# Two attention and gated-MLP layers on one core: score blocks tied to slots, products in column parts, weights transposed by their loads, and more units for VectorE

## The chip, the cores and the metric

The kernel runs on one core of a Trainium2 chip. A core has a matrix engine (TensorE, "PE" in the profile; its weight loads are shown as "PEld"), ScalarE ("ACT"), VectorE ("DVE"), GpSimd ("POOL") and a queue engine (SyncE, "SP") that issues the DMA transfers. The metric is the device time of one execution in microseconds (us). The kernel before took 1782.1, 1781.82 and 1775.51 us in three runs, a median of 1781.82 us.

## The reference, cut to what matters

There are 2048 tokens of width 512. Two layers follow each other with the same weights. Each layer is an attention part with 32 query heads of 16 elements that share one key and one value head, and then a gated MLP whose gate mixes the tokens with a 2048 x 2048 matrix `w_sp`.

```
scores = jnp.einsum('bhqd,bkd->bhqk', q, k) * Dh ** (-0.5)
p = _softmax(scores, axis=-1)
o = jnp.einsum('bhqk,bkd->bhqd', p, v)
...
z = _gelu(jnp.einsum('bsd,df->bsf', x, w_in))
z1 = z[..., :Fh].copy()
z2 = _layernorm(z[..., Fh:], axis=-1)
g = jnp.einsum('ts,bsf->btf', w_sp, z2) + b_sp[None, :, None]
return jnp.einsum('bsf,fd->bsd', z1 * g, w_out)
...
x = x + _A_ref(_layernorm(x, axis=-1), A_wq, A_wk, A_wv, A_wo)
x = x + _B_ref(_layernorm(x, axis=-1), B_w_in, B_w_sp, B_b_sp, B_w_out)
```

The softmax needs an exponential for each of 32 x 2048 x 2048 scores in each layer. In the kernel this is the largest piece of element work.

## The kernel before, in words

**Units, blocks and slots.** The scores of a layer are cut into 32 *groups* (2048 query rows each, counted over heads and tokens), and a group into 16 *units*, one for each tile of 128 keys. A unit is four *blocks* of 128 keys x 512 queries; block j lies in row part j of the array, because the contraction is only 32 rows deep (16 elements, and 16 that are zero). `scores` issues the matmul of one block with `tile_position=(32 * j, 0)`. Matmuls in different row parts run beside each other.

**Who makes the exponentials.** Most units go to ScalarE: `push_unit` queues their blocks, and `push_slot` puts them, three and two in turn, into two PSUM *slots* (banks 0 to 2 and 3 to 4); one `activation` call (line 805) turns a whole slot into probabilities in `P_ring`. `push_pv` then multiplies the unit's four blocks with the values (line 822), in four column parts of the array, into bank 6. Some units go to VectorE instead (`push_unit_dve`): each of the four blocks gets a bank of its own from the two *side banks* 5 and 7, line 853 turns the scores into 16-bit integers, four integer additions (line 862) make four shifted copies, and read as bf16 numbers the five copies, weighted by `PH_W`, sum to the exponential. Their product with the values (line 868) takes five sets of four matmuls where a ScalarE unit takes one. `ON_DVE` and `UNITS` say which units of a group go to VectorE: none in the first four groups (apart from `FIRST_DVE`), three of 16 in the next 20, two in the next four, one in the last four. That makes 152 of the 1024 units of both layers.

**The order of the work.** The program is first written as a graph of operations with priorities and estimated durations (`_Graph.op`), and `schedule` plays it through before anything is emitted, with the constants at the head of the file. Each engine then executes its own list strictly in that order, with semaphores between the engines (`emit`). On PE a set of up to four small matmuls, or one full 128 x 128 matmul, is charged 0.217 us for 512 columns. Each operation has a `mode`: 1 for row parts (scores), 2 for column parts (values), 0 for the full array, and a change of mode is charged 0.105 us. Where PE would be idle for long, `filler` puts in matmuls with ones or zeros (lines 613, 618 and 621) that change no result. The matmuls of a product are added in pieces by `products`; their banks are the side banks.

**Around the attention.** While the attention runs, the rest of the layer runs at lower priority: `q_slot` (queries, line 751), `wo_tiles` (output projection, line 950), `b_front` (the MLP's input products, lines 1020 and 1039), and `mix_stage` (the mixing of the tokens in three stages of four token tiles, line 1146, with sums parked in device memory, `gp_d`). After the last group of a layer, `mix_late` does the last stage (line 1185), the gating (line 1194) and the output product (line 1198). In the first layer this is interleaved with the first keys and scores of the second layer, and in the second layer it is the end of the kernel.

**The mixing matrix.** The product needs `w_sp` with its two dimensions swapped. In the first layer `turn_wsp` loads 16 row tiles of 512 KB, transposes them on PE (256 matmuls with the identity, line 1245), copies them out of PSUM on VectorE (32 copies, line 1248) and stores them to `wspt_scratch` in device memory. `mix_stage` (line 1127) and `mix_late` (line 1162) load from there, with 40 loads in both layers together. The weights `wo`, `w_in` and `w_out` are loaded between the row tiles (`load_weights`).

Of the kernel before, what the change touches and what calls it, by code (L numbers as in the profile page):

```python
# [17 lines left out]
KD = 4  # L18
# [86 lines left out]
class _Graph:  # L105
# [66 lines left out]
    def schedule(self):  # L172
# [81 lines left out]
        def pick(e):  # L254
# [7 lines left out]
            for ent in ready[e]:  # L262
# [3 lines left out]
                p = ent[0] - (0.95 if e == "pe" and o.mode == last_mode else 0.0)  # L266
                if beside(o):
                    p -= 2.0
# [191 lines left out]
def bass_interleave_layers__grouped_kv_mqa__mixer_gmlp__prompt_kernel(  # L460
# [98 lines left out]
    z1flat = z1c[:].rearrange("p f s -> p (f s)")  # L559
    wsp_stage = z1flat[:, 0:2 * S].rearrange("p (b s) -> p b s", b=2)  # L560
    wsp_tile = z1flat[:, 2 * S:4 * S].rearrange("p (b t q) -> p b t q", b=2, q=P)
    Z1ALL = [("z1", f, t) for f in range(NF1) for t in range(NT)]

    wspT_d = nc.dram_tensor("wspt_scratch", [NT, P, S], BF16)
    wspT_dv = wspT_d.ap().rearrange("st p t -> p st t")
# [22 lines left out]
    def dve(fn, us, r, w, prio=5):  # L588
        return op("dve", fn, us, r=r, w=w, prio=prio)

# [56 lines left out]
    def load_weights(i):  # L647

        rd = [("wd", 2 * i + 1)]
        if i == 0:  # L650
            dma(lambda e: e.dma_start(wo_r[:], A_wo.rearrange("(c p) n -> p c n", p=P)), rd, ["wo"], "wo", 6.0)
        elif i == 1:
            dma(lambda e: e.dma_start(w_in_r[:], B_w_in.rearrange("(kd p) f -> p kd f", p=P)), rd, ["w_in"], "win", 10.0)
        elif i == 2:
            dma(lambda e: e.dma_start(w_out_r[:], B_w_out.rearrange("(c p) n -> p c n", p=P)), rd, ["w_out"], "wout",
                10.0)
# [85 lines left out]
    def q_slot(si, pr=3):  # L742
# [5 lines left out]
        def mk(e, k):  # L748
            u, kd = k // KD, k % KD
            c = g // 2 * m + u  # L750
            return e.matmul(bank32(tk.bank)[:, u * w:(u + 1) * w], wq_r[:, kd, c * P:(c + 1) * P],  # L751
                            xnTA[:, kd, t0 * P:t0 * P + w], start=(kd == 0), stop=(kd == KD - 1))
        products(tk, m * KD, mk, lambda k: [("xa", k % KD, t) for t in range(t0, t0 + n)] + ["wq"], pr,
                 us=w * MM + 0.01)
# [7 lines left out]
    main = {"blocks": [], "i": 0, "s": 0, "pv": [], "last": None}  # L762
    SLOTS = ((0, 3), (3, 2))

    def push_unit(u):

        main["pv"].append([u, 4])
        for j in range(4):
            main["blocks"].append((u, j))
# [14 lines left out]
    def push_slot(n):  # L784
# [3 lines left out]
        main["i"] += 1  # L788
        b0 = SLOTS[i][0]
# [12 lines left out]
        o.rows = frozenset(j for _, j in blocks)  # L802

# [12 lines left out]
    def push_pv(u, places):  # L816
        hg, kt, first, last, done = u

# [6 lines left out]
        pv_op(pe_pv, [("P", s) for s, _ in places] + [("V", kt)], first, last, TILED)  # L825
        if last:
            done()
# [12 lines left out]
    def push_unit_dve(u):  # L840

        hg, kt, first, last = u[:4]
        assert not first and not last
        tiles = [phr["base"] + (phr["n"] + a) % NRING for a in range(NPH)]
        phr["n"] += NPH
        first_op = None
        for j in range(4):
            tk = _Task()
            o = op("pe", lambda e, j=j, tk=tk: scores(e, bank32(tk.bank), u, j), TILED, r=[("K", hg[1], kt), ("q", hg[0])],
                   w=[tk], prio=P_S, lat=PE_LAT, mode=1)  # L850
            o.work = TILED / 4
            o.rows = frozenset((j,))
            o = dve(lambda e, j=j, tk=tk: e.tensor_scalar(  # L853
                ph16[:, tiles[0], j * QC:(j + 1) * QC], bank32(tk.bank), PH_BIAS, 0.0, op0=ALU.add, op1=ALU.max),
                0.66, [tk], BIG(tiles[0]) if j == 0 else [("phj", tiles[0], j)], P_R)
            if j == 0:
                first_op = o
            else:
# [417 lines left out]
    for layer in range(2):  # L1276
        now["layer"] = layer
        phr["base"] = 8 - NRING
        for t0, n in KEYS:
# [12 lines left out]
            if not layer and t0 == 0:  # L1292
                for tt in range(NT):
                    turn_wsp(tt)
                    if tt % 2:
                        load_weights(tt // 2)
# [40 lines left out]
```

## Time and profile before

| what | value |
|---|---|
| runs | 1782.1, 1781.82 and 1775.51 us (median 1781.82) |
| span of the profiled execution | 1773.4 us; the page gives no other time for this execution |
| PE busy | 1689.0 us (95%), 15326 matmuls |
| ScalarE busy | 1663.7 us (94%), 1586.3 us of it the exponentials of line 805 |
| VectorE busy | 1355.8 us (76%) |
| GpSimd busy | 92.1 us (5%) |
| DMA | 133.00 MB, mean 75 GB/s |

The span runs from the first to the last instruction, so it lies a little below the times of the runs. A busy PE is not PE at its peak: matmuls are pipelined, and each record includes the time that it takes to pass through the array, so the time from one start to the next says more than a duration. The same holds for the exponentials, whose records overlap: 698 calls of 1528 ns and 696 calls of 1108 ns would be more than the 1586.3 us in which the engine was busy with them. "Idle before" is the time an engine stood still ahead of a group of instructions, with what ended it.

### The profile page before, as it was taken

The page shows a single profiled execution, that of the slowest core. Times are in us where ns is not written, and L with a number is a line of the kernel's source. Part 1 is how long each engine was busy: PE and PEld are TensorE (multiplying, and loading weights), DVE is VectorE, ACT ScalarE, POOL GpSimd, SP SyncE. Part 2 cuts the span into 40 slices and gives each one's busy share as a digit, 9 for nine tenths or more (in the row PEclk, how much of TensorE's full clock was granted, in tenths as well). Part 3 has the DMA queues.
Part 4 walks back from the last instruction along what each step waited for, and adds up shares of the span by engine and source line. Part 5 has one row for each costly group of instructions (what it writes and reads, how often), then busy time and mean ns, then how long its engine had stood idle before and what let it go on. Part 6 is the DMA issues. An engine that isn't in the chain of part 4 may idle for free.

```text
span 1773.4 us, 35455 instructions
## 1 busy us (share of the span) xinstructions
PE 1689.0 (95%) x15326; PEld 556.9 (31%) x15326; DVE 1355.8 (76%) x2450; ACT 1663.7 (94%) x1448; POOL 92.1 (5%) x145
## 2 busy tenths in 40 slices
PE   8899999999999999999999999999999999999999
PEld 4332322232333232233433222322232332322333
DVE  8679787888888877544677886888888887765647
ACT  7999999999999999999588999999999999999980
POOL 2000000000000000000322000000000000000012
PEclk9999999999999999999999999999999999999999
DMA  5840100011000223555420000001200003244474
GB/s 159 228 109 1 49 1 1 25 64 34 7 13 7 88 92 114 179 178 175 138 75 25 1 2 1 2 1 37 78 25 1 13 14 104 80 164 156 144 251 164
DMA packets 112044, 133.00 MB, mean 75 GB/s; under 512 B 41104, under 2 KB 68112, under 8 KB 111888
## 3 DMA queue, kind: packets, MB, share of 16 engines
q1 hardware_dynamic: 111888, 130.74, 22.8%
q8 instruction: 120, 1.97, 0.4%
q14 instruction: 36, 0.29, 0.0%
HBM read 76.19 MB, written 54.53 MB: 74 GB/s over the span
## 4 chain that ended last, share of the span: by engine, by line
ACT 77%; PE 20%; DVE 2%; DMA 1%; issue 1%; POOL 0%; SPq 0%; DVEq 0%
ACT P_ring L805 73%; PE ps_all L781 5%; PE ps_all L822 2%; PE ps_all L1146 2%; PE ps_all L1198 2%; PE ps_all L868 2%; PE ps_all L1185 1%; PE ps_all L1020 1%; ACT z2n L1063 1%; ACT z1c L1088 1%; PE ps_all L621 1%; ACT L805 1%; ACT L1063 1%; DMA z1c<-in_B_w_sp_dram 0%; PE ps_all L751 0%
## 5 line engine op out<-in xcount | busy, mean ns | idle before, releaser
L805 ACT ACTIVATE P_ring<-ps_all 128x1536 bf16<-128x1536 f32 (+1 forms) x1396 | 1586.3, 1317 | 58.2 <-PE ps_all L781 56.4
L781 PE MATMUL ps_all<-qT,kT_rep 32*128 32x512 bf16 x4096 | 640.4, 385 | 67.8 <-ACT P_ring L805 51.4
L853 DVE TENSOR_SCALAR big<-ps_all 128x512 int16<-128x512 f32 x608 | 400.0, 685 | 45.5 <-PE ps_all L781 40.0
L862 DVE TENSOR_SCALAR big<-big 128x2048 int16<-128x2048 int16 x608 | 396.9, 682 | 24.9 <-PE ps_all L868 23.6
L781 PEld LDWEIGHTS ps_all<-qT,kT_rep 32*128 32x128 bf16 x4096 | 159.1, 91 | 587.4 <-ACT P_ring L805 449.1
L822 PE MATMUL ps_all<-P_ring,V_aug 128*32 128x512 bf16 x3488 | 340.5, 390 | 2.1 <-DVE oT L916 1.1
L868 PE MATMUL ps_all<-big,V_ph 128*32 128x512 bf16 x3040 | 251.2, 388 | 0.6 <-DVE big L853 0.4
L1149 DVE TENSOR_TENSOR big<-ps_all,big 128x512 f32<-128x512 f32 x112 | 76.5, 687 | 105.3 <-PE ps_all L1146 105.0
L822 PEld LDWEIGHTS ps_all<-P_ring,V_aug 128*32 128x32 bf16 x3488 | 86.5, 93 | 190.7 <-issue 171.5
L621 PE MATMUL ps_all<-ones,zeros 128*32 128x512 bf16 x1400 | 122.9, 388 | 0.0
L868 PEld LDWEIGHTS ps_all<-big,V_ph 128*32 128x32 bf16 x3040 | 72.3, 96 | 89.4 <-issue 37.2
L679 POOL TENSOR_SCALAR ve<-mv 128x4 f32<-128x4 f32 (+3 forms) x38 | 11.2, 296 | 1615.1 <-DVE mv L692 1210.2
L943 DVE TENSOR_TENSOR X<-ps_all,X 128x512 bf16<-128x512 f32 x64 | 44.0, 687 | 36.7 <-PE ps_all L1198 19.3
L916 DVE CAST oT<-ps_all 128x512 bf16<-128x512 f32 x56 | 38.6, 690 | 38.7 <-PE ps_all L822 38.2
L1146 PE MATMUL ps_all<-z1c,z2n 128*128 128x512 bf16 x224 | 63.3, 383 | 0.0
L1146 PE MATMUL ps_all<-z2n 128*128 128x512 bf16 x224 | 63.0, 383 | 0.0
L1146 PE MATMUL ps_all<-xnTA,z2n 128*128 128x512 bf16 x224 | 60.6, 382 | 0.3 <-DVE big L1149 0.3
L1020 PE MATMUL ps_all<-w_in_r,xo 128*128 128x448 bf16 x256 | 60.2, 355 | 0.5
L1149 DVE TENSOR_TENSOR big<-ps_all,bsp 128x512 f32<-128x512 f32 x56 | 38.5, 688 | 27.5 <-PE ps_all L1146 27.3
L1198 PE MATMUL ps_all<-w_out_r,z1c 128*128 128x512 bf16 x224 | 54.9, 381 | 0.2 <-DVE X L943 0.2
L1029 DVE CAST z2n<-ps_all 128x448 bf16<-128x448 f32 x60 | 37.2, 622 | 23.1 <-PE ps_all L1020 21.5
L1039 PE MATMUL ps_all<-xo,w_in_r 128*128 128x512 bf16 (+3 forms) x336 | 53.8, 309 | 0.3 <-DVE z1c L1053 0.3
(88 smaller groups left out, 1087.6 us busy)
## 6 DMA issues: line engine op xcount, KB each, us to landing
gp_scratch<-big SPq DMA_DIRECT2D x168, 256.0 KB, 2.1
big<-gp_scratch SPq DMA_DIRECT2D x154, 256.0 KB, 3.1
z1c<-in_B_w_sp_dram SPq DMA_DIRECT2D x16, 512.0 KB, 5.3
wspt_scratch<-z1c SPq DMA_DIRECT2D x16, 512.0 KB, 5.5
z2n<-wspt_scratch SPq DMA_DIRECT2D x8, 512.0 KB, 3.9
z1c<-wspt_scratch SPq DMA_DIRECT2D x8, 512.0 KB, 3.8
big<-wspt_scratch SPq DMA_DIRECT2D x8, 512.0 KB, 4.1
big<-gp_scratch SPq DMA_DIRECT2D x28, 128.0 KB, 2.6
```

The source lines that it names most:

```text
L621: ins = e.matmul(bank32(PVB)[32 * j:32 * j + 32, :], zeros[:, 0:32], mv, tile_position=(0, 32 * j), start=False, stop=False)
L781: return e.matmul(out, kT_rep[32 * j:32 * j + 32, a, u[1] * P:(u[1] + 1) * P], qT[32 * j:32 * j + 32, q, :], tile_position=(32 * j, 0), st ...
L805: return e.activation(P_ring[:, s0:s0 + n, :], bank32(b0, n).rearrange("p (k q) -> p k q", k=n), ACTF.Exp, scale=E_SCALE)
L822: ins = e.matmul(bank32(PVB)[32 * j:32 * j + 32, :], V_aug[:, kt, :], P_ring[:, s, :], tile_position=(0, 32 * j), start=first, stop=last)
L853: o = dve(lambda e, j=j, tk=tk: e.tensor_scalar(ph16[:, tiles[0], j * QC:(j + 1) * QC], bank32(tk.bank), PH_BIAS, 0.0, op0=ALU.add, op1=AL ...
L862: dve(lambda e, a=a: e.tensor_scalar(ph16[:, tiles[a], :], ph16[:, tiles[0], :], float(PH_A[a]), None, op0=ALU.add), 0.63, base, BIG(tiles ...
L868: ins = e.matmul(bank32(PVB)[32 * j:32 * j + 32, :], V_ph[:, a, kt, :], big[:, tiles[a], j * QC:(j + 1) * QC], tile_position=(0, 32 * j), ...
L1020: products(tk, KD, lambda e, kd, i=i, h=h, tk=tk: e.matmul(bank32(tk.bank)[:, 0:448], xo[:, kd, i * P:(i + 1) * P], w_in_r[:, kd, FH + h * ...
L1039: return e.matmul(bank32(tk.bank)[:, a * w:(a + 1) * w], w_in_r[:, kd, (f0 + a) * P:(f0 + a + 1) * P], xo[:, kd, c0:c0 + w], start=(kd == ...
L1146: return e.matmul(bank32(tk.bank), z2n[:, a0 + s, ft * P:(ft + 1) * P], rows_of(s)[0], start=(s == 0), stop=(s == nb - 1))
L1149: dve(lambda e, part=part, tk=tk: e.tensor_tensor(part, bank32(tk.bank), part if st else bsp[:], ALU.add), 0.69, [tk] + ([] if st else ["b ...
L1198: products(tk, NF1, lambda e, ft, t=t, tk=tk: e.matmul(bank32(tk.bank), z1c[:, ft, t * P:(t + 1) * P], w_out_r[:, ft, :], start=(ft == 0), ...
```

## The change

The change has these parts.

1. **Score blocks of VectorE.** `push_unit_dve` is gone. `plan` lists ahead of time which units of a group go to VectorE and at which count of ScalarE's blocks each of their blocks is due (15 blocks ahead of an even spread). `push_slot` calls `apart` after each slot. It takes a due block whose row part the slot does not use, and `block_dve` makes its score matmul depend on the slot's matmuls. `finish_units` issues what is left before a group's last unit, and `sum_units` issues the five products of a unit once its group is open. In the scheduler the matmuls of a slot get a priority that is higher by 5.
2. **Products in column parts.** `side4` issues a product of 128 x 128 weights as four matmuls with 32 columns of weights each, with `mode=2`. It is used for the queries, the output projection, the MLP's input products and the mixing, and in `mix_late` of the first layer from token tile 4 on. The full matmul stays for the queries of single-tile chunks, for the last token tile's products (`fine`, `G.chain`), for the first two steps of `mix_late` in the first layer and for all of it in the second.
3. **Mixing weights.** `turn_wsp` and `wspt_scratch` are gone. The 40 loads read `B_w_sp` itself with `transpose=True`. `load_weights` issues the three weight loads after the input.
4. **More units for VectorE.** In each layer groups 24 to 27 go from two units to three, and groups 28 to 31 from one to two: 16 units more, 168 in all.

```diff
+                if e == "pe" and o.task is not None and o.task.slot is not None:
+                    p -= 5.0
...
+    def side4(e, out, w, mv, start, stop):
+        ins = None
+        for j in range(4):
+            ins = e.matmul(out[32 * j:32 * j + 32, :], w[:, 32 * j:32 * j + 32], mv, tile_position=(0, 32 * j),
+                           start=start, stop=stop)
+        return ins
...
-            return e.matmul(bank32(tk.bank)[:, u * w:(u + 1) * w], wq_r[:, kd, c * P:(c + 1) * P],
-                            xnTA[:, kd, t0 * P:t0 * P + w], start=(kd == 0), stop=(kd == KD - 1))
+            mul = side4 if n > 1 else PE_FULL
+            return mul(e, bank32(tk.bank)[:, u * w:(u + 1) * w], wq_r[:, kd, c * P:(c + 1) * P],
+                       xnTA[:, kd, t0 * P:t0 * P + w], kd == 0, kd == KD - 1)
...
+    def apart(slot_op):
+        missing = [j for j in range(4) if j not in slot_op.rows]
+        while spread["todo"]:
+            x = spread["todo"][0]
+            if x["at"][x["n"]] > main["n"]:
+                return
+            j = next((j for j in missing if j in x["left"]), None)
+            if j is None:
+                return
+            missing.remove(j)
+            block_dve(x, j, slot_op)
...
+        o = op("pe", lambda e: scores(e, bank32(tk.bank), u, j), TILED, r=[("K", hg[1], kt), ("q", hg[0])],
+               w=[tk], prio=P_S, lat=PE_LAT, mode=1)
+        if slot_op is not None:
+            o.deps[slot_op] = 0
...
-            dma(lambda e, a=a, m=m, rows=rows: e.dma_start(rows[:, 0:m, :], wspT_dv[:, a0 + a:a0 + a + m,
-                                                                                   tc * QC:(tc + 1) * QC]),
-                [("wd", tt) for tt in range(NT)], keys, chan, 5.0)
+            dma(lambda e, a=a, m=m, rows=rows: e.dma_start(
+                rows[:, 0:m, :], B_w_sp[tc * QC:(tc + 1) * QC, (a0 + a) * P:(a0 + a + m) * P], transpose=True),
+                [], keys, chan, 4.0 + 0.5 * m)
...
-            products(tk, nb, mk, lambda s: Z2(a0 + s) + rows_of(s)[1], pr, per=2)
+                return side4(e, bank32(tk.bank), z2n[:, a0 + s, ft * P:(ft + 1) * P], rows_of(s)[0], s == 0, s == nb - 1)
+            products(tk, nb, mk, lambda s: Z2(a0 + s) + rows_of(s)[1], pr, per=2, mode=2)
...
+        mul, mode = (side4, 2) if layer == 0 and t0 >= LATE4 else (PE_FULL, 0)
...
-    def turn_wsp(tt):
...
+    LATE4 = 4
+    LEAD = 15
...
-    ON_DVE = [0] * NFIRST + [3] * (24 - NFIRST) + [2] * 4 + [1] * 4
+    ON_DVE = [0] * NFIRST + [3] * (28 - NFIRST) + [2] * 4
```

## The prediction

> **What bounds the kernel now.** I read the busy times first, then the costliest groups, the stretches of the span, the waits, and last a piece of the timeline for the pitch of PE's matmuls. The busy times and the largest groups:
>
> ```profile
> PE 1689.0 (95%) x15326; PEld 556.9 (31%) x15326; DVE 1355.8 (76%) x2450; ACT 1663.7 (94%) x1448; POOL 92.1 (5%) x145
> ...
> ACT 77%; PE 20%; DVE 2%; DMA 1%; issue 1%; POOL 0%; SPq 0%; DVEq 0%
> ...
> L805 ACT ACTIVATE P_ring<-ps_all 128x1536 bf16<-128x1536 f32 (+1 forms) x1396 | 1586.3, 1317 | 58.2 <-PE ps_all L781 56.4
> L781 PE MATMUL ps_all<-qT,kT_rep 32*128 32x512 bf16 x4096 | 640.4, 385 | 67.8 <-ACT P_ring L805 51.4
> L853 DVE TENSOR_SCALAR big<-ps_all 128x512 int16<-128x512 f32 x608 | 400.0, 685 | 45.5 <-PE ps_all L781 40.0
> L862 DVE TENSOR_SCALAR big<-big 128x2048 int16<-128x2048 int16 x608 | 396.9, 682 | 24.9 <-PE ps_all L868 23.6
> ...
> L822 PE MATMUL ps_all<-P_ring,V_aug 128*32 128x512 bf16 x3488 | 340.5, 390 | 2.1 <-DVE oT L916 1.1
> L868 PE MATMUL ps_all<-big,V_ph 128*32 128x512 bf16 x3040 | 251.2, 388 | 0.6 <-DVE big L853 0.4
> ...
> L621 PE MATMUL ps_all<-ones,zeros 128*32 128x512 bf16 x1400 | 122.9, 388 | 0.0
> ```
>
> PE and ScalarE both look full. But PE's records include fillers (L621), and the chain that ended last is 77% ScalarE. The stretches, with the columns span, PE, PEld, DVE, ACT and POOL busy, decide between them:
>
> ```profile
> 100.00:850.00 750.00, 721.02 (x6657) 226.76 (x6656) 575.92 (x1030) 740.46 (x644) 13.73 (x20) 0.99 0.20 65
> 850.00:950.00 100.00, 94.90 (x717) 39.87 (x714) 73.08 (x147) 68.66 (x62) 36.95 (x51) 1.00 0.28 91
> 950.00:1707.00 757.00, 724.83 (x6775) 224.81 (x6773) 584.85 (x1045) 750.77 (x654) 12.71 (x20) 1.00 0.17 58
> 1707.00:1773.40 66.40, 60.70 (x307) 26.90 (x305) 50.57 (x81) 16.03 (x15) 16.50 (x16) 1.00 0.51 178
> ```
>
> In the two attention stretches ScalarE stands still for 9.5 of 750 and 6.2 of 757 us. It is the bound there. Its other idle time is the start (11.9 us of the first 50), the change of layers (31.3 us of 850 to 950) and the tail (50.4 us), where PE and its chain with VectorE set the pace.
>
> For PE's true load I take the pitch, from one start to the next:
>
> ```profile
> 405.00 0.40 PE L822 MATMUL ps_all<-P_ring,V_aug 128*32 128x512 bf16 x4
> 405.23 0.60 PE L868 MATMUL ps_all<-big,V_ph 128*32 128x512 bf16 x8
> 405.66 0.39 PE L822 MATMUL ps_all<-P_ring,V_aug 128*32 128x512 bf16 x4
> 405.98 0.61 PE L1146 MATMUL ps_all<-z1c,z2n 128*128 128x512 bf16 x2
> 406.52 0.40 PE L781 MATMUL ps_all<-qT,kT_rep 32*128 32x512 bf16 x4
> ```
>
> Two sets of L868 in four column parts take 405.66 - 405.23 = 0.43 us, so 0.215 us a set. L822 followed by a full product takes 0.32 us, so the change of shape costs 0.105 us. Two full matmuls and a change take 0.54 us, 0.217 us each. Over the program as built (sets of up to four column or row parts at 0.215 us for 512 columns, narrower ones in proportion, nothing under 0.06 us, the pitch of the 128-wide transposes) that makes 1241.6 us of sets, 90.3 of them fillers, and 3277 changes or 344.1 us: 1585.7 us of a span of 1773.4.
>
> **The change, part by part.**
>
> *16 more units for VectorE.* 64 blocks leave ScalarE. A block costs it 1586.3 / 3488 = 0.4548 us, so 64 x 0.4548 = 29.1 us go, all in the last eight groups of each layer, where ScalarE is the bound (49.9 of 50 us in 1600 to 1650). VectorE gets 64 of L853 (400.0 / 608 = 0.658 us) and 64 of L862 (0.653 us): 83.9 us, half in each layer. It was busy for 114 us of 650 to 850, so about 156 of 200 after: covered. If that cover were gone, a unit of 5.2 us would have to fit into the time of a group (25 us) beside the other work, and PE would wait for its banks. PE gets five sets where it had one, 64 x 0.215 = 13.8 us.
>
> *Score blocks tied to slots.* A block alone costs a set and often two changes; in a row part that the slot leaves free it runs beside it. Counted in the built programs, score sets fall from 1574 to 1497, 16.6 us less. The wait is in PE's order alone: behind the block stands the next slot, and if neither side bank is free, that slot and then ScalarE wait. Before, PE's loads waited for L853 104 times, for 34.4 us in all. The blocks now come spread out and no longer four in a row, so I leave this at nothing; doubled, it would be 34 us of PE time.
>
> *Column parts.* 1700 sets replace as many full matmuls at the same 0.215 us, and stand in the same shape as the value products. The changes fall from 3277 to 2883, 41.4 us less. 328 of the sets are 256 wide. No row shows such a set: its bounds are 0.108 us (in proportion) and 0.215 us (the wide set), 35 us of PE in all between them. I take 0.108, since the four weight loads of a set show 86.5 / 872 = 0.099 us together. PE's instructions grow from 15322 to 20301 matmuls.
>
> The Trainium skill (TensorEngine Tiling, Restrictions and Gotchas) speaks against this part: column tiling excludes the fast weight load. By that rule, with the four loads of 93 ns one behind the other, a set would take 0.372 us and PE gain 267 us; the trace, with 0.215 us from set to set and 0.099 us for four loads, does not agree, and the sum goes by the trace.
>
> *Mixing weights.* Out go 16 loads, 16 stores, 256 transposes on PE (15.4 us) and 32 copies on VectorE (21.8 us), all in the first 200 us, where ScalarE is busy already: worth nothing by itself. The 40 loads stay 40, but each transposes 512 KB (or 384 and 128). No row shows such a load. The near end is the plain one of before, 3.8 to 4.1 us to landing; the far end is one packet for each element: the queue's 111888 packets took 22.8% of 16 engines' 1773.4 us, 57.8 ns each, so 262144 of them 947 us. The plan allows 4.0 + 0.5 us for each of four tiles, 6 us. I take the near end, because the program holds one instruction for each load, as before, and the same bytes move. What stands behind them on SP's queue are the parked sums (182 loads, 168 stores), two or three products ahead; they and the three weight loads, now issued with the input, are needed late.
>
> The Trainium skill has two rules on this. One (Advanced Engine Details and Errata, DGE: Hardware vs Software) rates transposes on the hardware queues as the worse kind; the other (DMA: Bandwidth & Descriptors, Latency and other measured facts) gives 261 GB/s, from which I estimate 2.0 us for 512 KB. No run here shows either yet.
>
> *What PE has left.* In all PE falls from 1585.7 to 1220.6 + 302.7 = 1523.3 us. The tightest place is the last eight groups of a layer:
>
> | last eight groups | PE, us | ScalarE's blocks x 0.4548, us |
> |---|---|---|
> | first layer, before / after | 194.5 / 186.8 | 198.3 / 194.7 |
> | second layer, before / after | 194.7 / 183.9 | 198.3 / 192.9 |
>
> So ScalarE stays the bound with more room under it (cut at the transposes of finished groups, these stretches do not hold quite the same work). PE, next in line, was 98% full there already and cost ScalarE almost nothing.
>
> *The idle time of ScalarE.* Of the 15.7 us in the attention stretches I take a quarter off, 4 us, for PE's room and the slots' priority (bounds 0 and 15.7). At the change of layers PE's work falls by 3.1 us (140.4 to 137.3 without fillers in the first four groups of the second layer); I take 3 us (bounds: 6 more, since all queries now stand ahead of the first scores, and 10 less). Start and tail keep their work: PE in the tail 57.0 to 55.7 us, taken as 0.
>
> The sum: -29.1 - 4 - 3 = -36 us, so a span of 1737. The page gives the profiled execution no time but its span, which lies 8.4 us below the median of the runs and 2.1 below the fastest; I carry the 8.4 over: 1781.8 - 36 = 1746 us.
>
> **The rivals.**
>
> *Slower: the transposing loads land late.* PE stands in order at the first mixing matmul, and ScalarE has two slots, 2.3 us, in hand. Landing within 6 + 2.3 us costs nothing. At 36 / 40 = 0.9 us beyond, 9.2 us on average, the gain is gone. At 12 us with half of them exposed, 20 x 3.7 = 74 us come on top: 1820 us. For it: nothing shows such a load, and late mixing is what the planner's figures decide. Against: plain loads land in 4 us and DMA engines are 20% busy in the attention. The skill's 261 GB/s bears against it, its other rule for it.
>
> *Slower: column parts pay for their loads.* At 0.372 us a set PE needs 1523 + 267 = 1790 us and becomes the bound: about 1840 with the 50 us of waits of start and change. It decides from about 0.34 us a set (PE beyond ScalarE's span). 1982 such sets ran before at 0.215.
>
> *No change: PE waits for the side banks.* If 672 tied blocks hold up their slots by half of the 0.33 us that a wait took before (34.4 / 104), and a third of it reaches ScalarE, 672 x 0.055 = 37 us come back: 1783 us. For it: two banks for all side work, VectorE at 81% of the span. Against: such waits were covered before.
>
> *Faster by less: narrow sets cost 0.215 us.* 35 us more on PE, most in the queries and the first halves of the layers, where PE has room; a third reaches the change of layers: 1758 us.
>
> **How the numbers follow.** The forecast has 0.68, narrow sets 0.13, side banks 0.07, late loads 0.10, loads of column parts 0.02. The range goes down to 1732, with the bounds of idle time, and up to 1773 over the narrow sets; what lies above is the side banks' and the slower cases, some 0.15, below 0.04. Half a per cent, 9 us, is about what a measurement of this kernel tells from no change. Faster: 0.68 + 0.13 + a little of the side banks, 0.83; same 0.05; slower 0.12.
>
> **What the profile after would show.** ScalarE: 3424 blocks, some 1557 us in L805's successor at 0.455 a block, and still over 98% busy in the attention. VectorE: 672 and 672 of the two groups. PE: 32-wide products at 0.215 us from set to set, and no waits of PE for a DMA. Mixing loads: 4 to 6 us to landing. The prediction is wrong if ScalarE's idle time in the attention grows from 16 us to over 50, if PE's list shows waits behind mixing loads or side banks, or if the change of layers takes visibly more than its 31 us.

## The result and the profile after

The changed kernel takes 1749.43 us (median of 4 runs, 1744.55 to 1750.24), the kernel before 1781.96 us beside it (4 runs, 1775.51 to 1782.23). The ratio is 0.9825, with a 95% interval of 0.9803 to 0.9847. The forecast was 1746 us, with a range of 1732 to 1773. The profiled execution took 1749.69 us, with a span of 1747.8 us.

The page of the kernel after, busy times, chain and largest groups (the groups' columns: busy time and mean ns of one, then the engine's idle time ahead of them and what ended it):

```profile
PE 1625.6 (93%) x20292; PEld 548.7 (31%) x20305; DVE 1404.2 (80%) x2546; ACT 1633.5 (93%) x1422; POOL 95.2 (5%) x145
...
ACT 77%; PE 19%; DVE 2%; issue 1%; POOL 0%; DMA 0%; SPq 0%; DVEq 0%
...
L810 ACT ACTIVATE P_ring<-ps_all 128x1536 bf16<-128x1536 f32 (+1 forms) x1370 | 1555.8, 1336 | 61.7 <-PE ps_all L784 60.8
L784 PE MATMUL ps_all<-qT,kT_rep 32*128 32x512 bf16 x4096 | 600.7, 385 | 91.5 <-ACT P_ring L810 81.7
L902 DVE TENSOR_SCALAR big<-ps_all 128x512 int16<-128x512 f32 x672 | 450.7, 685 | 116.6 <-PE ps_all L784 110.7
L913 DVE TENSOR_SCALAR big<-big 128x2048 int16<-128x2048 int16 x672 | 438.1, 680 | 1.7 <-PE ps_all L927 0.3
...
L627 PE MATMUL ps_all<-ones,zeros 128*32 128x512 bf16 x1256 | 105.2, 388 | 0.0
```

ScalarE's busy time falls by 30.2 us, from 1663.7 to 1633.5; the exponentials alone fall by 30.5 (1586.3 to 1555.8 us), about the 29.1 us forecast for 64 blocks. The span falls by 25.6 us, from 1773.4 to 1747.8. The rest, 30.2 - 25.6 = 4.6 us, is more idle time of ScalarE. The stretches show where (span, PE, PEld, DVE, ACT, POOL busy, granted clock, DMA share, GB/s), cut around the change of layers and at 1681 us, where the second layer's exponentials end:

```profile
100.00:840.00 740.00, 697.66 (x8832) 228.92 (x8833) 618.48 (x1108) 728.74 (x634) 17.03 (x22) 0.99 0.21 63
840.00:950.00 110.00, 99.90 (x1462) 43.96 (x1464) 76.99 (x158) 74.91 (x67) 37.47 (x51) 0.98 0.29 70
950.00:1681.00 731.00, 686.20 (x8800) 219.76 (x8800) 612.77 (x1095) 726.39 (x633) 12.33 (x18) 1.00 0.20 60
1681.00:1747.80 66.80, 57.44 (x300) 26.15 (x306) 48.13 (x76) 15.54 (x14) 16.28 (x16) 1.00 0.61 172
```

ScalarE is busy for 98.5% and 99.4% of the two attention stretches: it is still the bound there. The change of layers is not shorter: measured from the last exponential of the first layer to the end of the last long wait for scores, ScalarE idles for 34.5 us there (before: 31.4). The tail, from the last exponential to the end, is 66.5 us (before: 65.5).

### The profile page after: what moved, and what is told of

Read it like the earlier page. It is cut to its first block, busy times and chain, and to the rows that moved or that the text cites. A ratio compares the mean times of both kernels' runs of the same rounds, so it can differ in the third digit from the quotient of the medians.

```text
span 1747.8 us, 45403 instructions
## 1 busy us (share of the span) xinstructions
PE 1625.6 (93%) x20292; PEld 548.7 (31%) x20305; DVE 1404.2 (80%) x2546; ACT 1633.5 (93%) x1422; POOL 95.2 (5%) x145
## 4 chain that ended last, share of the span: by engine, by line
ACT 77%; PE 19%; DVE 2%; issue 1%; POOL 0%; DMA 0%; SPq 0%; DVEq 0%
ACT P_ring L810 74%; PE ps_all L593 6%; PE ps_all L784 5%; PE ps_all L587 3%; PE ps_all L927 2%; PE ps_all L829 2%; ACT z1c L1146 1%; ACT z2n L1121 1%; DVE big L1247 0%; PE ps_all L627 0%; ACT L810 0%; ACT L1121 0%; DVE xn L697 0%; DMA X<-in_A_x_dram 0%; PE ps_all L942 0%
## 5 line engine op out<-in xcount | busy, mean ns | idle before, releaser
L810 ACT ACTIVATE P_ring<-ps_all 128x1536 bf16<-128x1536 f32 (+1 forms) x1370 | 1555.8, 1336 | 61.7 <-PE ps_all L784 60.8
L784 PE MATMUL ps_all<-qT,kT_rep 32*128 32x512 bf16 x4096 | 600.7, 385 | 91.5 <-ACT P_ring L810 81.7
L902 DVE TENSOR_SCALAR big<-ps_all 128x512 int16<-128x512 f32 x672 | 450.7, 685 | 116.6 <-PE ps_all L784 110.7
L913 DVE TENSOR_SCALAR big<-big 128x2048 int16<-128x2048 int16 x672 | 438.1, 680 | 1.7 <-PE ps_all L927 0.3
L927 PE MATMUL ps_all<-big,V_ph 128*32 128x512 bf16 x3360 | 309.0, 387 | 2.2 <-DVE big L902 1.3
L927 PEld LDWEIGHTS ps_all<-big,V_ph 128*32 128x32 bf16 x3360 | 81.7, 94 | 129.3 <-issue 54.9
L593 PE MATMUL ps_all<-z2n 128*32 128x512 bf16 x896 | 65.5, 383 | 0.8 <-DVE big L1206 0.5
L593 PE MATMUL ps_all<-xnTA,z2n 128*32 128x512 bf16 x896 | 64.9, 381 | 1.0 <-DVE big L902 0.5
L593 PE MATMUL ps_all<-z1c,z2n 128*32 128x512 bf16 x896 | 64.1, 381 | 0.6 <-DVE big L1206 0.3
L1002 DVE TENSOR_TENSOR X<-ps_all,X 128x512 bf16<-128x512 f32 x64 | 43.8, 685 | 23.4 <-PE ps_all L593 11.2
L593 PE MATMUL ps_all<-w_in_r,xo 128*32 128x448 bf16 x960 | 60.9, 354 | 0.6 <-DVE xo L708 0.5
L593 PE MATMUL ps_all<-xo,w_in_r 128*32 128x512 bf16 (+2 forms) x1120 | 53.4, 327 | 1.4 <-DVE z1c L1111 1.2
L1252 POOL TENSOR_TENSOR z1c<-big,z1c 128x512 bf16<-128x512 f32 (+1 forms) x47 | 44.9, 968 | 67.7 <-DVE big L1247 65.2
```

The lines of the kernel that those rows point to most:

```text
L593: ins = e.matmul(out[32 * j:32 * j + 32, :], w[:, 32 * j:32 * j + 32], mv, tile_position=(0, 32 * j), start=start, stop=stop)
L784: return e.matmul(out, kT_rep[32 * j:32 * j + 32, a, u[1] * P:(u[1] + 1) * P], qT[32 * j:32 * j + 32, q, :], tile_position=(32 * j, 0), st ...
L810: return e.activation(P_ring[:, s0:s0 + n, :], bank32(b0, n).rearrange("p (k q) -> p k q", k=n), ACTF.Exp, scale=E_SCALE)
L902: o = dve(lambda e: e.tensor_scalar(ph16[:, tiles[0], j * QC:(j + 1) * QC], bank32(tk.bank), PH_BIAS, 0.0, op0=ALU.add, op1=ALU.max), 0.66 ...
L913: dve(lambda e, a=a: e.tensor_scalar(ph16[:, tiles[a], :], ph16[:, tiles[0], :], float(PH_A[a]), None, op0=ALU.add), 0.63, base, BIG(tiles ...
L927: ins = e.matmul(bank32(PVB)[32 * j:32 * j + 32, :], V_ph[:, a, kt, :], big[:, tiles[a], j * QC:(j + 1) * QC], tile_position=(0, 32 * j), ...
```

## The experiments

In the first four runs, theory 1 takes each part for itself, as the prediction did; theory 2 lets the room on TensorE decide. From the fifth on, theory 1 is what the first four suggested: that what decides is how much of the mixing is left when a layer's scores end. The experiments were timed on three chips (e1 to e4, e5 to e8, e9 to e12), each beside the kernel before. So differences below are differences of the ratios to the kernel before, times 1782 us; the changed kernel was not timed again beside them, and a difference of a few us from it lies within the two intervals.

For each kernel the table gives the ratio, the products of the mixing's three background stages that stand behind the last scores of layer 1 and of layer 2 in TensorE's list (*late*; 336 belong to each layer, 168 in e6 and e7), and ScalarE's idle time at the change of layers and the length of the tail in the profiled execution.

| kernel | ratio (95%) | late, layers 1 / 2 | idle at change, us | tail, us |
|---|---|---|---|---|
| before | 1 | 24 / 26 | 31.4 | 65.5 |
| after | 0.9825 (0.9803 to 0.9847) | 0 / 8 | 34.5 | 66.5 |
| e1 units alone | 1.0310 (1.0276 to 1.0344) | 94 / 100 | 69.4 | 103.9 |
| e2 all but the units | 1.0027 (1.0008 to 1.0047) | 0 / 0 | 34.5 | 66.2 |
| e3 full products | 0.9992 (0.9974 to 1.0010) | 38 / 44 | 43.8 | 80.5 |
| e4 scratch back | 0.9861 (0.9832 to 0.9890) | 12 / 0 | 31.6 | 66.2 |
| e5 blocks back in fours | 1.0249 (1.0210 to 1.0289) | 88 / 78 | 71.7 | 101.8 |
| e6 before, half the mixing | 1.0034 (1.0017 to 1.0051) | 0 / 0 | 40.5 | 66.2 |
| e7 units, half the mixing | 0.9841 (0.9813 to 0.9868) | 2 / 6 | 34.4 | 66.7 |
| e8 eight more units | 0.9944 (0.9922 to 0.9966) | 34 / 58 | 44.4 | 80.7 |
| e9 no slot priority | 0.9835 (0.9786 to 0.9884) | 0 / 10 | 34.5 | 66.1 |
| e10 late part in full products | 0.9851 (0.9811 to 0.9892) | 0 / 0 | 32.9 | 66.7 |
| e11 each load twice | 0.9832 (0.9791 to 0.9874) | 0 / 8 | 35.0 | 69.0 |
| e12 blocks start later | 0.9864 (0.9825 to 0.9904) | 0 / 0 | 34.9 | 66.2 |

For layer 1 the expectations below count only the late products that stand ahead of layer 2's first scores: 38 in e1, 26 in e3 and 34 in e5. In these three kernels 56, 12 and 54 more stand behind those scores. The mixing's background products of e1 after the last scores of layer 1, up to layer 2's first scores at 854 us and behind them (the second number is TensorE busy, its count in brackets):

```profile
822.00:854.00 32.00, 10.03 (x38) 3.23 (x36) 1.00 0.59 189
854.00:900.00 46.00, 15.75 (x56) 5.62 (x56) 0.96 0.76 252
```

### One part alone, or one part undone

**e1: the kernel before with the 16 units alone.**

```diff
-    ON_DVE = [0] * NFIRST + [3] * (24 - NFIRST) + [2] * 4 + [1] * 4
+    ON_DVE = [0] * NFIRST + [3] * (28 - NFIRST) + [2] * 4
```

> The kernel before with only its table of units changed: 16 units more for VectorE, nothing else. Theory 1 (ScalarE's count of blocks is what the span follows): 29 us less than before, about 1753 us, with ScalarE's exponentials at about 1557 us. Theory 2 (PE, 98% full in the last eight groups, has no room for 16 more units without the other parts): the 13.8 us of value products and the extra score sets and changes of shape come out as idle time of ScalarE, and less than half of the gain stays, 1768 us or more.

It took 1831.74 us against 1776.85: 55 us *slower*. Theory 1 falls. Theory 2's bound of 1768 us holds, but it had a smaller gain in mind and no loss. The exponentials shrank as forecast (1558.4 us), and they ended earlier: layer 1's at 822.5 us, against 838.3 in the kernel before. But the change of layers and the tail each became 38 us longer. The longest wait of ScalarE at the change, and then the chain in the tail (by line, and a piece of it: start, duration, what):

```profile
913.11 1.02 ACT L805 ACTIVATE P_ring<-ps_all 128x1024 bf16<-128x1024 f32 x1 [44.16 <-PE ps_all L781]
```

```profile
by line: DMA gp_scratch<-big 27.5%; PE ps_all L1198 22.7%; DMA big<-gp_scratch 8.2%; issue 6.5%; PE ps_all L1146 5.1%; PE ps_all L1185 4.6%; DVE big L1189 3.5%; DVE big L1149 3.4%; POOL z1c L1194 2.2%; PE ps_all L613 1.8%; PE ps_all L1020 1
...
1741.59 0.69 DVE big L1149
1742.30 5.14 DMA gp_scratch<-big
1747.45 3.77 DMA big<-gp_scratch
1751.31 0.70 DVE big L1149
1752.03 5.31 DMA gp_scratch<-big
```

L1146 is the mixing's background product. After it VectorE adds the parked sum (L1149), the sum is stored to `gp_scratch`, and the next stage or the late part has to load it again. A store and a load of 256 KB take 3.5 to 5.4 us each here, one behind the other. They are 35.7% of the 104 us of this chain: 37 us, nearly all of the 38 us by which the tail grew. At the change they are less: 14 us of the chain from 823 to 967 us. In the tail of the kernel before, the chain has no transfer among its larger pieces:

```profile
by line: PE ps_all L1198 32.3%; PE ps_all L1185 19.5%; ACT z1c L1088 14.6%; DVE big L1189 7.7%; issue 7.4%; DVE z1c L1194 5.8%; DVE X L943 2.0%; ACT L1088 1.9%; DVE st L1097 1.8%; POOL rs L681 0.9%; DVE z2n L1104 0.8%; ACT z2n L1025 0.7%; P
```

**e2: the changed kernel with the old number of units.** The edit of e1 the other way round, made on the kernel after.

> The changed kernel with the old table of units (152 instead of 168): tied score blocks, column parts and transposing loads remain. Theory 1: only what PE's relief gives, 0 to 7 us less than the kernel before, 1775 to 1782 us. Theory 2: PE's relief carries the gain, 1765 us or less.

1782.12 us against 1776.85, ratio 1.0027: 5 us slower. The tied blocks, the column parts and the transposing loads together bring nothing without the units. Theory 2 falls; theory 1's small gain of up to 7 us did not come either.

**e3: the changed kernel with full products.**

```diff
 def side4(e, out, w, mv, start, stop):
-        ins = None
-        for j in range(4):
-            ins = e.matmul(out[32 * j:32 * j + 32, :], w[:, 32 * j:32 * j + 32], mv, tile_position=(0, 32 * j), ...)
-        return ins
+        return PE_FULL(e, out, w, mv, start, stop)
...
-            products(..., mode=2)
+            products(..., mode=0)
```

> The changed kernel with every product as one full matmul again (mode 0). Some 390 changes of shape or more come back, 41 us of PE time. Theory 1: ScalarE still bounds the attention and PE has some 90 us of fillers and idle time over it, so at most 8 us are lost, 1750 to 1758 us. Theory 2: PE is full again in the tightest groups and most of 41 us shows, 1770 us or more.

1776.03 us against 1776.85, ratio 0.9992: without the column parts the whole gain is gone, which is theory 2's. Layer 1's exponentials end as early as in the changed kernel (821.0 us, there 824.8); the change of layers idles 9.3 us longer and the tail is 14.0 us longer. Its tail's chain holds parked sums again:

```profile
by line: PE ps_all L587 56.8%; DMA big<-gp_scratch 10.9%; DMA gp_scratch<-big 6.3%; DVE big L1243 4.6%; issue 4.5%; DVE z1c L1248 4.4%; DVE big L1202 4.4%; DVE X L998 1.6%; PE ps_all L615 1.5%; DVE oT L971 0.9%; PE ps_all L825 0.4%; PE ps_a
```

17.2% of 80.5 us are 13.8 us, what the tail has grown by.

**e4: the changed kernel with the mixing matrix turned on TensorE and kept in device memory.** `turn_wsp`, `wspt_scratch` and the old loads and `load_weights` are back.

```diff
-            dma(lambda e, ...: e.dma_start(rows[:, 0:m, :], B_w_sp[tc * QC:(tc + 1) * QC, ...], transpose=True), [], ...)
+            dma(lambda e, ...: e.dma_start(rows[:, 0:m, :], wspT_dv[:, a0 + a:a0 + a + m, tc * QC:(tc + 1) * QC]),
+                [("wd", tt) for tt in range(NT)], ...)
```

> The changed kernel with the mixing matrix transposed on PE and loaded from the scratch, as before. 16 loads, 16 stores, 256 transposes on PE (15.4 us) and 32 copies on VectorE (21.8 us) come back in the first 200 us. Theory 1 (covered there): within 4 us of the changed kernel, 1746 to 1754 us. Theory 2 (PE and VectorE have no room there either): 8 us or more lost, 1757 us or more, with ScalarE's idle time between 50 and 200 us of the span grown by as much.

1752.83 us, ratio 0.9861: 6 us above the changed kernel's, with intervals that overlap. The time lies in theory 1's range, the 6 us between the 4 of theory 1 and the 8 of theory 2. ScalarE's idle time from 50 to 200 us is 5.2 us, 3.6 more than in the changed kernel, and 4.5 us of it lie in windows of 10 us with a lowered granted clock. So the loads are worth little; whether it is nothing isn't settled.

**e5: the changed kernel with VectorE's blocks in fours again.** `push_unit_dve`, `attn_first` and `attn_rest` of the kernel before are back; units, column parts and loads stay.

```diff
-                if kt - t0 not in on_dve:
-                    push_unit((q_of(gi), kt, kt == t0, kt == t0 + n - 1, done))
+                u = (q_of(gi), kt, kt == t0, kt == t0 + n - 1, done)
+                if kt - t0 in on_dve:
+                    push_unit_dve(u)
+                else:
+                    push_unit(u)
```

> The changed kernel with VectorE's score blocks in fours again, one unit's four blocks straight after one another and not tied to ScalarE's slots; units, column parts and transposing loads stay. Theory 1 (ScalarE's saving counts only if TensorE has finished the mixing's products before the last scores of the layer): in this kernel's order 34 of these products lie behind the last scores of layer 1 and 78 behind those of layer 2 (0 and 8 in the changed kernel, 26 and 44 with full products, which cost 24 us, 38 and 100 with the units alone, which cost 80 us), so about 1800 us, between those two, and the time is lost at the change of layers and in the tail. Theory 2 (ScalarE's count and TensorE's sum of set times decide): 77 more score sets are 16.6 us of TensorE, which still has 130 us of slack over the whole run, so within 5 us of the changed kernel, 1750 to 1755 us.

1824.57 us against 1776.42, ratio 1.0249: 76 us slower than the changed kernel. Tying the blocks, which the prediction valued at 16.6 us of TensorE time and no time of the kernel, carries more than any other part. Theory 1 is right in place and missed the size by 25 us. The longest wait of ScalarE, and the chain by line over the stretch from the last exponential of layer 1 to the end of that wait (823 to 926 us):

```profile
925.70 4.62 ACT L810 ACTIVATE P_ring<-ps_all 128x1024 bf16<-128x1024 f32 x4 [52.90 <-PE ps_all L784]
```

```profile
by line: DMA big<-gp_scratch 23.6%; PE ps_all L593 15.3%; DMA gp_scratch<-big 12.3%; PE ps_all L587 10.2%; PE ps_all L1315 4.5%; DVE big L1285 4.4%; PE ps_all L1321 3.6%; issue 3.0%; DVE xn L697 2.7%; DVE X L1036 2.5%; PE ps_all L704 2.1%; 
```

Parked sums make up 35.9% of 103 us, 37 us; ScalarE's idle time at the change is 40.3 us above that of the kernel before. In the changed kernel the same stretch shows no transfer among its larger pieces.

How far the mixing is at 800 us shows it before the loss is felt. These are the instructions that read or write `z2n`, from 300 to 800 us (the second number is PE busy, its count in brackets: full products before and in e1, four column parts for each product after and in e5). Before, after, e1, e5:

```profile
300.00:800.00 500.00, 75.68 (x272) 18.87 (x272) 30.09 (x55) 6.38 (x2) 0.99 0.21 71
```

```profile
300.00:800.00 500.00, 90.65 (x1248) 27.81 (x1248) 28.49 (x50) 8.83 (x3) 0.99 0.27 82
```

```profile
300.00:800.00 500.00, 60.99 (x216) 14.44 (x216) 30.69 (x55) 6.38 (x2) 1.00 0.17 55
```

```profile
300.00:800.00 500.00, 63.65 (x912) 20.59 (x912) 32.54 (x58) 6.72 (x3) 1.00 0.20 58
```

Of 336 products 272, 1248 / 4 = 312, 216 and 912 / 4 = 228 are done, and the layer's last exponential ends 38, 25, 22 and 22 us later.

### Is it the work that runs beside the attention?

If the units pay only when the mixing is done in time, they must pay on the old kernel too, once the mixing is small.

**e6: the kernel before, with half the mixing's background products**, as control:

```diff
-                                stop=(s == nb - 1))
-            products(tk, nb, mk, ...)
+                                stop=(s == nb // 2 - 1))
+            products(tk, nb // 2, mk, ...)
```

> The kernel before, with each of the mixing's three background stages computing two of its four products instead of four (168 products of 512 columns less in each layer, 336 x 0.215 = 72 us of TensorE; the loads, the sums and the parking in device memory stay; the output is not the reference's). It is the control for the next run. Theory 1: ScalarE's count is unchanged and the mixing was nearly done in time in the kernel before (24 and 26 products late), so a gain of 0 to 15 us: 1762 to 1777 us. Theory 2 (TensorE is in the way all along): a gain of half to all of the 72 us: 1705 to 1740 us.

1782.93 us against 1776.42, ratio 1.0034. TensorE lost 72 us of products and the kernel gained nothing. Theory 2 falls; theory 1's range is missed too, since 6 us were lost (at the change one wait is 18.6 us long; why this list has it was not followed up). About half of the time went into fillers, on the page of e6:

```profile
L621 PE MATMUL ps_all<-ones,zeros 128*32 128x512 bf16 x2048 | 169.4, 385 | 0.0
```

They were 1400 matmuls and 122.9 us in the kernel before: 648 more, 162 sets, 35 us at 0.215 us each.

**e7: the same with the 16 units of e1, and nothing else of the change.**

> The same with the 16 more units of VectorE (the unit counts of the changed kernel), nothing else of the change. Its order has 2 and 6 of the mixing's products behind the last scores of the layers. Theory 1: with TensorE's background out of the way the units bring their 29 us: 29 (23 to 35) us less than the kernel with half the mixing, where on the full mixing they cost 55 us. Theory 2 (the units in themselves hurt, through VectorE or through the rows that blocks in fours leave unused): no less than the kernel with half the mixing, within 5 us or slower.

1751.12 us, ratio 0.9841: 31.8 us faster than e6, where theory 1 had 29 (23 to 35). The same edit that costs 55 us on the full mixing brings 32 us on half of it. So the units in themselves do not hurt, and what takes their gain goes with the mixing's background products. No run takes 72 us of other work from TensorE, so whether it must be the mixing's is argued from the chains of e1 and e5.

**e8: the changed kernel with eight more units**, three in each of the last four groups of both layers.

```diff
-    ON_DVE = [0] * NFIRST + [3] * (28 - NFIRST) + [2] * 4
+    ON_DVE = [0] * NFIRST + [3] * (32 - NFIRST)
```

> The changed kernel with 3 units on VectorE in the last four groups of each layer too, in place of 2: 8 more units, 32 blocks x 0.454 = 14.5 us less on ScalarE. Theory 1: its order has 34 and 58 of the mixing's products behind the last scores, so the gain is lost again: 1770 to 1800 us, slower than the changed kernel, the loss at the change and in the tail. Theory 2 (ScalarE's count decides): 1749 - 14 = 1735 us.

1768.52 us against 1776.42, ratio 0.9944, about 21 us slower than the changed kernel. ScalarE's exponentials fell to 1542.4 us, 13.4 less, and idle time at the change (44.4) and the tail (80.7) took more than that back. Theory 1 had a loss, 1.5 us larger at least; theory 2's 1735 is excluded.

### The smaller pieces

**e9: without the slots' priority.**

```diff
-                    p -= 5.0
+                    p -= 0.0
```

> The changed kernel without the priority of 5 that puts ScalarE's slots ahead of all other work on TensorE in the written order; all else stays. Theory 1 (the parts of the change matter through the mixing's products that are late at the end of a layer): 0 and 10 of them are late in this order, as in the changed kernel (0 and 8), so 1750 to 1756 us. Theory 2 (the priority is what keeps ScalarE fed): ScalarE's idle time in the attention rises from 16 us by half or more and the time is 1762 us or above.

1753.05 us, ratio 0.9835, 2 us from the changed kernel's: theory 1. The priority is not what matters. (ScalarE's idle time in the attention is 23.5 us in this profile, nearly theory 2's half more; 10.5 us of it lie in windows of 10 us with a granted clock under 0.985, 6.2 us in the changed kernel.)

**e10: the late mixing of the first layer in full products.**

```diff
-    LATE4 = 4
+    LATE4 = 16
```

> The changed kernel with the late mixing and the last product of the first layer (the part that runs inside the second layer, up to the change) in full products again instead of column parts; the background stages keep column parts. No product of the mixing is late (0 and 0). Theory 1 (column parts pay only where the mixing's background stages run against their end): no difference, 1746 to 1755 us. Theory 2 (every full product among blocks costs its two changes of shape): about 320 products in 160 pairs, up to 160 x 0.11 = 17 us of TensorE, and in the stretch after the change, where TensorE is nearly full, up to half of it is seen: 1755 to 1760 us.

1754.47 us, ratio 0.9851, 5 us above the changed kernel's with overlapping intervals. It lies in theory 1's range, half a microsecond from theory 2's, and so tells them apart no further; column parts matter little there, at any rate against the 30 us of e3.

**e11: each transposing load twice in a row, into the same place.**

```diff
+            for _ in range(2):
-            dma(lambda e, ...: e.dma_start(rows[:, 0:m, :], B_w_sp[...], transpose=True), ...)
+                dma(lambda e, ...: e.dma_start(rows[:, 0:m, :], B_w_sp[...], transpose=True), ...)
```

> The changed kernel with each of the 40 transposing loads issued twice in a row into the same place, so that the rows are there 8 us after the first issue instead of 4 and the sync engine's queue is held twice as long. The prediction put the point from which late loads decide at 9.2 us. Theory 1 (the loads are hidden with room to spare): 1747 to 1756 us. Theory 2 (the 4 us are just enough): the mixing's products wait for their rows, and they run against their end, so 1765 us or more.

1750.74 us, ratio 0.9832: 1 us. The loads have room to spare. The only sign in the profile is two waits of TensorE for them, 2.6 and 0.5 us, and a tail of 69.0 us.

**e12: VectorE's blocks start 10 of ScalarE's blocks ahead instead of 15.**

```diff
-    LEAD = 15
+    LEAD = 10
```

> The changed kernel with VectorE's tied blocks starting 10 of ScalarE's blocks ahead of their place instead of 15. The number of blocks, sets and changes of shape is within a few of the changed kernel's, and no product of the mixing is late (0 and 0). Theory 1 (the products that are late decide): 1745 to 1752 us. Theory 2 (the place of VectorE's blocks in the order matters by itself: VectorE's three later steps of a unit and its sums come too late, and ScalarE's slots and the sums stand behind them): 1760 to 1775 us.

1756.74 us, ratio 0.9864: 7 us above the changed kernel's, between the two theories' ranges. With no product late at all it is not faster; ScalarE idles for 13.9 us in the second layer's attention (5.4 in the changed kernel), so a small part may hang on the place of the blocks, though the two intervals overlap. A configuration that beats the changed kernel was not found among these.

## Why the prediction was right, point by point

The time and the units' price were right. What the working had wrong is what the other parts are for: it took them as relief of TensorE worth some 4 to 7 us, and without either of two of them the gain is gone. The number came out because the change that was priced has all of them in it.

**The units.** 64 blocks x 0.4548 = 29.1 us were right: 30.5 measured in the exponentials, 31.8 us between e6 and e7. But the working let them stand by themselves, with TensorE as the next in line that "cost ScalarE almost nothing". By themselves they cost 55 us (e1). What was named for the case that VectorE's cover is gone, waits of TensorE for its banks, hardly grew (loads for scores waited 40.9 us for L853 in e1, 34.4 before); what came due was the background mixing.

**The parts that were to make room.** Each was priced by TensorE's time: 16.6 us for tied blocks, 41.4 us of changes of shape for the column parts, and then nearly nothing of it was put into the sum. Without the units this is right (e2: nothing; e6: 72 us less of products, nothing). With the units it is not: without the tied blocks 76 us are lost, without the column parts 30. The parts cannot be added: the four taken away one at a time, in the order of the changes above, lose 76, 30, 6 and 36 us, together 148, and all of them together 31. The table of the last eight groups (TensorE 98% full before) was the place to see this: the units shorten a layer by some 15 us and put sets of their own there, and what does not fit goes behind the last scores.

**What late products cost.** The tail is 65.5 to 69.0 us in all ten kernels with up to 26 late products in layer 2, 80.5 and 80.7 with 44 and 58, 101.8 and 103.9 with 78 and 100. Up to 26 are hidden in a chain that waits for other work anyway. Beyond that, stores and loads of parked sums stand in the chain of the tail: 13.9 us in e3 and 8.7 in e8, 31.7 in e5 and 37.1 in e1. At the change ScalarE idles for 31.4 to 40.5 us in the ten kernels with up to 24 late products in layer 1, 44.4 and 43.8 us with 34 and 38 (e8, e3), 71.7 and 69.4 us with 88 and 94 (e5, e1). What the idle time there consists of differs: parked sums make up 37 us of the chain in e5 and 14 in e1. So the number is a sign and no price list.

**ScalarE's idle time: the step that failed.** -4 us in the attention and -3 at the change of layers were forecast. The attention stayed at 16 us (11.0 + 5.4 after, 9.8 + 6.2 before), the change grew by 3.1 us, the tail by 1.0. At the change, the first wait went from 12.46 to 13.18 us with all the queries ahead of the first scores, and the last one from 5.16 to 10.90 us: a column-part product of 28 sets stands in front of the keys. The form of the product is not the cause (with full products there, e10, the last wait was 13.79 us). That the change of layers takes more than its 31 us was one of the prediction's own signs of being wrong, and it came, by 3 us. From the chain of the changed kernel, the queries' 16 sets and that product:

```profile
849.98 1.96 PE ps_all L593 x64
...
924.11 6.26 PE ps_all L593 x112
```

**The sum.** The span was forecast as 1737 us and came out as 1747.8: ScalarE's busy time gave 1.1 us more than forecast, and its idle time went 11.6 us the other way (+4.6 for -7). The 8.4 us that the profiled execution of before lay under its median were carried over; after, the profiled span lies only 1.6 us under the median. The two errors meet, and 1746 against 1749.43 looks better than the working was. Part of both errors lies in the pair of executions: the profiled one of before was the fastest of its four (1775.51 us), the one of after was not (1749.69, fastest 1744.55). Fastest against fastest, the gain is 31.0 us, so some 5 of the 11.6 us may be no work of the change; the 3.1 us at the change of layers can be seen in single waits.

**The rivals.** *Late loads* fall: landing took 3.6 to 5.8 us (medians by target; near end, 3.8 to 4.1), TensorE waits for no transfer, and doubling them costs 1 us (e11). From the issues of the kernel after (us to landing last):

```profile
xnTA<-in_B_w_sp_dram SPq DMA_TRANSPOSE x16, 3.6
z2n<-in_B_w_sp_dram SPq DMA_TRANSPOSE x8, 4.1
z1c<-in_B_w_sp_dram SPq DMA_TRANSPOSE x8, 4.2
big<-in_B_w_sp_dram SPq DMA_TRANSPOSE x8, 5.8
```

The Trainium skill (Advanced Engine Details and Errata, DGE: Hardware vs Software) rates transposes on the hardware queues as the worse kind; its next section (X-Bar Transpose (TRN2)) calls them as fast as plain transfers. The landing of these loads of up to 512 KB agrees with the second for three targets (`z2n` and `z1c` 4.1 and 4.2 us, plain ones before 3.9 and 3.8; `xnTA` 3.6, before 4.1 and 4.5) and not for `big` (5.8 us, before 4.1); the queue, below, shows a cost that neither names. The 2.0 us estimated from its other page (DMA: Bandwidth & Descriptors, Latency and other measured facts) are half of what was measured.

*Column parts that pay for their loads* and *narrow sets* fall by the pitch. The timeline of the kernel after (start, duration):

```profile
405.52 0.60 PE L593 MATMUL ps_all<-z1c,z2n 128*32 128x512 bf16 x8
406.06 0.51 PE L784 MATMUL ps_all<-qT,kT_rep 32*128 32x512 bf16 x4
```

```profile
849.98 1.93 PE L593 MATMUL ps_all<-xnTA,wq_r 128*32 128x256 bf16 x64
...
851.85 0.61 PE L721 MATMUL ps_all<-xnTA,wk_rep 128*128 128x256 bf16 x4
```

Two sets and a change take 0.54 us, as two full products did. Sixteen sets of 256 columns take at most 851.85 - 849.98 = 1.87 us, 0.117 each: near the 0.108 taken.

*Side banks.* TensorE's weight loads waited for VectorE's reads 58 times for 18.7 us, before 104 times for 34.4: right that tied blocks bring no new wait for the side banks. The loads for VectorE's own products (L927, before L868) now wait longer for it, 44.4 us against 22.2; ScalarE's idle time in the attention does not show it.

**What stays open.** Why blocks in fours make the mixing late is not shown. It is not TensorE's time alone. The fillers from 1500 to 1700 us, in the changed kernel and in e5:

```profile
1500.00:1700.00 200.00, 4.86 (x60) 1.22 (x60) 1.00 0.46 140
```

```profile
1500.00:1700.00 200.00, 14.74 (x172) 3.95 (x172) 0.98 0.28 86
```

In e5 43 sets of zeros stand in this stretch while 78 products will be late, and in the changed kernel 15 (in the kernel before 38, with 26 late). In the written order a filler is put in only where nothing else could be issued, so the products lacked something else: the two side banks, for which four blocks stand in a row, are the likely cause, but no run gave them a bank more. Nor does a run separate TensorE's time from bank time in what the column parts bring.

## What to carry to other kernels

An engine that is the bound can be relieved only as far as the work that hides beneath it still ends in time: count that work, see how much is left when the cover ends, and price what is left by its own chain (here 3.5 to 5.4 us for each transfer of a parked sum in it), not by its engine time. A busy engine with fillers has room and may still not be able to use it: making the background cheaper on a list that is in time anyway (e6) buys nothing, and the same relief is all that counts once the cover is shortened. So parts of such a change are tested in pairs, with and without the other, and not added up.

## What the runs showed of the hardware

A transposing load lands about as soon as a plain one for three of the four targets (above), but it holds the sync engine's queue longer. From the timeline of the kernel after (start, duration), a plain load and a transposing one:

```profile
519.82 0.32 SPq L1200 DMA_DIRECT2D big<-gp_scratch  x1
...
545.31 2.63 SPq L1185 DMA_TRANSPOSE z2n<-in_B_w_sp_dram  x1
```

The forty held it for 1.1 to 6.6 us each (the longest is the first, at 5 us); all other issues took 0.32 us in the median and 1.5 at most. What is issued behind them starts that much later; with 40 of them in 1748 us it did not matter, and neither did 80 (e11).

Short dips of the granted clock reach ScalarE. In these windows, of the kernel after and of e2, the granted clock (third number from the end) is 0.67 and 0.50, and ScalarE is busy for only 6.91 and 7.03 of 10 us:

```profile
300.00:310.00 10.00, 10.00 (x94) 2.35 (x87) 7.39 (x14) 6.91 (x7) 0.00 (x0) 0.67 0.01 2
```

```profile
1320.00:1330.00 10.00, 10.00 (x65) 1.56 (x62) 5.56 (x10) 7.03 (x6) 1.73 (x2) 0.50 0.01 2
```

Outside the change of layers and the tail, the windows of 10 us with a granted clock under 0.985 held 4.9 us of ScalarE's idle time in the kernel before, 6.2 after and 13.4 in e2, so differences of a few us between two profiled executions may be no more than that.
